# An FFT mixer followed by two MLPs: when the conversions, the transform's sums and the residual's stores are issued

## The chip, the core and the metric

The program runs on one NeuronCore of a Trainium2 chip. The metric is the device time of one execution in microseconds, lower is better. The engines are TensorE (PE), VectorE (DVE), ScalarE (ACT), GpSimd (POOL) and SyncE (SP). Each takes its own instructions strictly in the order in which the program emits them, and waits for semaphores of the others.

## The reference

Three layers follow one another on `x` of 4 x 3136 x 256, in float32:

```python
X = np.fft.rfft(x, axis=1)                         # along the 3136 tokens
x = np.fft.irfft(X * (filt_r + 1j * filt_i), n=3136, axis=1)

h = x.transpose(0, 2, 1) @ U @ V                   # rank 32, along the tokens
u = x + h.transpose(0, 2, 1)
x = u + np.maximum(u @ w_ch1, 0) @ w_ch2           # 256 -> 1024 -> 256

xn = (x - mean) / sqrt(var + 1e-6) * g_ln          # over the 256 channels
out = x + np.maximum(xn @ w_ch1b, 0) @ w_ch2b
```

U, V and the four MLP weights arrive as 64-bit floats, read as pairs of 32-bit words.

## The kernel before

**The arithmetic.** Products that need more precision than one float32r pass are done in three: each operand is split into a high and a low half, and `three` (lines 198 to 201) sums high x high, high x low and low x high on PE. So nearly every tensor has a high half, copied by ACT, and a low half, which DVE subtracts.

**The transform.** `fft(b)` (lines 277 to 357) treats batch b = 1 to 3 as a generator of 36 ticks. The batch's 3136 tokens are 14 pairs of 224 rows. Tick 1 loads; in the first stage (ticks 2 to 16) a tick splits pair i (`split`, lines 296 to 301), multiplies pair i - 1 (`mm1`), and writes the result `ze` to DRAM; POOL's queue loads the tables `ct` (`loadc`, line 290). In the second stage (ticks 19 to 35) a tick splits pair i, multiplies pair i - 1 (`mm2`, lines 313 to 321), whose `filt` (lines 217 to 228) makes `xs` (two copies by ACT, a product by POOL) and `ya` (a product by DVE); then `total` (lines 230 to 237) adds `xs` to `ya` of pair i - 2 on DVE, copies the sum to `yh` on ACT, and subtracts the rest `yl` on DVE; and `back` (lines 239 to 260) multiplies pair i - 3 by the inverse table into `ps`, copies it to `be` on ACT and stores that to `bd[b]`. Tick 36, `finish`, sets `tstk[b]`, from which on units of batch b may be loaded. Batch 0 is transformed ahead of the main loop by other code (class `First`).

**The main loop** (lines 960 to 990) is an order written out by hand. The tokens are 25 blocks of 512 (the last of 256). Each block k has a phase a (first MLP) and a phase b (second MLP), in the order a0 a1 a2 b0 b1 a3 b2 a4 b3 and so on; a phase has 8 steps, one for each 128 of the 1024 hidden channels, 400 steps in all. Step `idx` emits `m1` (six matmuls into `psh`, then ACT's `hh` and DVE's `hl`), `load_to`, perhaps one tick of the transform, the actions of `todo` that are due, and `m2` of step idx - 2, whose last one ends the phase (`end`, lines 655 to 696). In steps 3 and 6 of a phase a, one unit may follow (`unit`, lines 589 to 610): it takes 448 tokens of the transform's result from `bd` to channel-major `ah` and `al` by PE (`psu`), ACT and DVE. The kernel loads a unit (`load_unit`, lines 584 to 587: `ic`, then `wt`) once its batch's `tstk` is set. The first unit of batch 1, unit 7, is due in step 75, and emitting it advances the transform as far as it must.

**The transform's pace** (lines 971 to 975): after step FFT0 = 26 each step adds RATE = 0.75 to a credit while batch 1 is not done, and 0.4 later; when the credit reaches 1, a tick is emitted. Tick 1 falls in step 28, tick 36 in step 74.

**After a phase a** the sum x2 of MLP and residual is finished over the next steps by `todo` entries: DVE's transposes of its halves 3 and 4 steps later (line 675), `x2store` right behind the second one, four transfers to `xd` on SP's queue (lines 698 to 703), `x2load` 4 steps after that (line 708), then statistics on DVE (lines 710 to 734). Phase b ends with DVE's `x2t` (line 686) and the stores of `out` on SP.

**The conversions.** The weights are converted from 64-bit words by generators `to32` (lines 751 to 769). One job goes in segments: ACT writes `h` and `lf`; DVE's `words` makes `t`; POOL multiplies `lf` by `h` and adds it to `t`, named `ct`; `keep(t)` copies the high half (ACT; for w1b a DVE product `wg`, line 832); `last(t)` subtracts the low half, on POOL once `aside` is POOL (line 906), for w2b on DVE. `stagger` (lines 774 to 808) advances all live jobs by one segment per call and, once `brisk` is set just ahead of the main loop (line 961), starts a job every two calls. `CALLS` gives the calls: three in step 0, two in step 1, then one a step up to step 23.

Of the kernel before, what the change touches and what calls it, by code (L numbers as in the profile page):

```python
# [20 lines left out]
P = 128  # L21
# [22 lines left out]
PARTS, UPARTS = (0, 1, 2, 5, 6, 8), 10  # L44
CALLS = (0, 0, 0, 1) + tuple(range(1, 24))
LEAD = 3
FFT0, RATE = 26, 0.75

XTURN, XREAD, XSTAT, XROOT = (3, 4), 8, (10, 11), 12
BW = 32  # L50
# [88 lines left out]
def fft_mixer_kernel(ctx: ExitStack, tc: tile.TileContext, x, U, V, flt, w1, w2, gln, w1b, w2b,  # L139
                     c_fwd32, c_d32, c_e32, c_fwd, c_inv, c_e, c_d, c_w, out):  # L140
    nc = tc.nc
# [21 lines left out]
    def f32(ap):  # L163
        return ap.bitcast(F32)

    def acopy(o, i, scale=1.0):
        nc.scalar.activation(out=o, in_=i, func=AF.Copy, scale=scale)  # L167

    def sub(o, a, b):
        nc.vector.tensor_tensor(out=o, in0=a, in1=b, op=ALU.subtract)  # L170
# [14 lines left out]
    xd = [dram.tile([BLK, D], F32, name=f"xd{k}") for k in range(NBLK)]  # L185
# [6 lines left out]
    NCH = NM // 2  # L192

    def wide(dt, tag, name, w, bufs=2):
        t = fp.tile([PP, 2 * (D + R)], dt, tag=tag, name=name, bufs=bufs)
        return t[:, :2 * w].rearrange("p (a d) -> p a d", a=2)

    def three(o, lh, ll, rh, rl):
        nc.tensor.matmul(o, lh, rh, start=True, stop=False)  # L199
        nc.tensor.matmul(o, lh, rl, start=False, stop=False)  # L200
        nc.tensor.matmul(o, ll, rh, start=False, stop=True)  # L201

    def flat(t):
        return t.rearrange("p a d -> p (a d)")
# [72 lines left out]
    def fft(b):  # L277
        xv = x[b].rearrange("(p m) d -> p m d", m=NM)
        zw = zd[b].rearrange("(q m) w -> q m w", m=NM)
        zr = zd[b].rearrange("(g p) w -> p g w", p=PP)  # L280
        sp = Spectrum(b)
        live, tab, halves = {}, {}, {}

        def load1(i):
            live[i] = wide(F32, "fin", "xt", D, 3)
            nc.sync.dma_start(live[i], xv[:, 2 * i:2 * i + 2, :])

        def loadc(i):
            tab[i] = fp.tile([PP, 2, 2, PP], F32R, tag="ct", name="ct", bufs=2)
            nc.gpsimd.dma_start(tab[i], c_fwd[:, 2 * i:2 * i + 2])  # L290

        def load2(i):
            live[i] = wide(F32, "fin", "zt", D, 3)
            nc.sync.dma_start(live[i], zr[:, 2 * i:2 * i + 2, :])

        def split(i):
            xt = live.pop(i)
            hi, lo = wide(F32R, "fhi", "hi", D), wide(F32R, "flo", "lo", D)
            acopy(hi, xt)
            sub(lo, xt, f32(hi))  # L300
            halves[i] = hi, lo

        def mm1(i):
            ct = tab.pop(i)
            hi, lo = halves.pop(i)
            ze = wide(F32, "fev", "ze", D)
            ps = ps_m.tile([P, 512], F32, tag="m", name="ps1")
            for m in range(2):
                three(ps[:PP, m * D:(m + 1) * D], ct[:, m, 0], ct[:, m, 1], hi[:, m], lo[:, m])
            acopy(flat(ze), ps[:PP])  # L310
            nc.sync.dma_start(zw[:, 2 * i:2 * i + 2, :], ze)

        def mm2(i):
            hi, lo = halves.pop(i)
            ps = ps_m.tile([P, 512], F32, tag="m", name="ps2")
            if i == 0:
                for g in range(2):
                    three(ps[:, g * D:(g + 1) * D], e_sb[:, 1 - g, 0], e_sb[:, 1 - g, 1], hi[:, g], lo[:, g])
            else:
                three(ps, e_sb[:, 0, 0], e_sb[:, 0, 1], flat(hi), flat(lo))  # L320
            sp.filt(i, ps)

        load1(0)
        load1(1)
        loadc(0)
        yield
        for i in range(NCH + 1):
            if i < NCH:
                split(i)
            if i > 0:  # L330
                mm1(i - 1)
            if i + 2 < NCH:
                load1(i + 2)
            if i + 1 < NCH:
                loadc(i + 1)
            yield
        load2(0)
        load2(1)
        sp.load(0)
        for _ in range(2):  # L340
            yield
        for i in range(NCH + 3):
            if i < NCH:
                split(i)
            if 0 < i <= NCH:
                mm2(i - 1)
            if 1 < i <= NCH + 1:
                sp.total(i - 2)
            if i > 2:
                sp.back(i - 3)  # L350
            if i + 2 < NCH:
                load2(i + 2)
            if i + 1 < NCH:
                sp.load(i + 1)
            yield
        sp.finish()
        yield
# [216 lines left out]
    def blen(k):  # L574
        return min(BLK, NTOK - k * BLK)
# [122 lines left out]
    def x2store(k, x2):  # L698

        n = blen(k)  # L700
        for i in range(P // BW):
            nc.sync.dma_start(xd[k].rearrange("(j t) (i c) -> t j i c", t=BW, i=P // BW)[:, :n // BW, i],
                              x2[i * BW:(i + 1) * BW, :n // BW].rearrange("p j c k -> p j (c k)"))

    def x2load(k):
# [37 lines left out]
    def words(s, h, t):  # L743

        hb, tb = h.bitcast(I32), t.bitcast(I32)
        nc.vector.tensor_scalar(out=h, in0=h, scalar1=TOP, scalar2=None, op0=ALU.min)
        nc.vector.tensor_scalar(out=tb, in0=hb, scalar1=3, scalar2=None, op0=ALU.logical_shift_left)
        nc.vector.scalar_tensor_tensor(out=tb, in0=s[:, :, 1], scalar=-0x80000000, in1=tb, op0=ALU.bitwise_and, op1=ALU.bitwise_or)
        nc.vector.tensor_scalar(out=hb, in0=tb, scalar1=-0x800000, scalar2=None, op0=ALU.bitwise_and)

    def to32(i, s, keep, last):


        p, n = s.shape[:2]
        tags = ("xs", "ya") if brisk and i % 2 else ("yh", "yl")
        h, lf = (fp.tile([P, 512], F32, tag=tag, name=f"c{tag}", bufs=3 if tag == "ya" else 2)[:p, :n] for tag in tags)
        nc.scalar.activation(out=h, in_=s[:, :, 1].bitcast(F32), func=AF.Abs, scale=2.0 ** -112)
        nc.scalar.activation(out=lf, in_=s[:, :, 0].bitcast(U32), func=AF.Copy, scale=2.0 ** -52)
        yield
        t = fp.tile([P, 2 * (D + R)], F32, tag=("fhi", "flo")[i % 2], name="ct", bufs=2)[:p, :n]  # L760
        words(s, h, t)
        yield
        nc.gpsimd.tensor_tensor(out=lf, in0=lf, in1=h, op=ALU.mult)
        nc.gpsimd.tensor_tensor(out=t, in0=t, in1=lf, op=ALU.add)
        yield
        keep(t)
        yield
        last(t)
        yield

    after = []
    aside, brisk = nc.vector, False

    def stagger(jobs):

        words, live, fetched = {}, [], 0
        after.clear()

        def fetch(n):
            nonlocal fetched  # L780
            while fetched < min(n, len(jobs)):
                words[fetched] = jobs[fetched][0]()
                fetched += 1

        def advance():
            nonlocal live
            while after:
                after.pop()()
            live = [g for g in live if next(g, 0) is None]

        for n in range(4):
            fetch(n + 1)
            yield
        for i in range(len(jobs) + 4):
            if brisk:
                advance()
            if i < len(jobs):
                live.append(to32(i, words.pop(i), *jobs[i][1:]))
                next(live[-1])
            yield  # L800
            advance()
            if brisk:
                fetch(i + 3)
            yield
            if not brisk:
                advance()
                fetch(i + 3)
                yield
# [73 lines left out]
    with tc.manual_schedule():  # L882
# [6 lines left out]
        def chain():  # L889
            for b in range(1, NB):  # L890
                yield from fft(b)

        first = First()
        pr = stagger([w_job("w1", w1, 0, "wt"), w_job("w1", w1, 1, "wt"), v_job(0), v_job(1)] + [w_job(nm, w, j) for nm, w, j in (
            ("w2", w2, 0), ("w1", w1, 2), ("w1", w1, 3), ("w2", w2, 1), ("w2", w2, 2),
            ("w2", w2, 3), ("w1b", w1b, 0), ("w1b", w1b, 1), ("w2b", w2b, 0), ("w1b", w1b, 2), ("w1b", w1b, 3),
# [64 lines left out]
        brisk = True  # L961
# [61 lines left out]
```

## Time and profile before

| | |
|---|---|
| median of 3 runs | 1402.79 us (1402.31 to 1405.51) |
| the profiled execution | 1402.46 us, its span 1400.7 us |
| PE busy | 1358.4 us (97%), 7678 matmuls |
| DVE, ACT, POOL busy | 802.0 (57%), 549.8 (39%), 173.9 us (12%) |
| granted clock of PE, mean | 0.989 |
| the chain that ended last | PE 82%, DVE 4%, ACT 2%, DMA 1% |
| DMA | 152.29 MB, mean 109 GB/s |

The profile is of one execution; the sum in the prediction is made against that one's 1402.46 us. Matmuls overlap one another, so PE's busy time is a union of overlapping spans: where it is full, a matmul follows the last without a gap, and where it is not, PE waited. "A <- B" says that A stood idle until B's instruction was done. A wait of an engine that is not late for anything costs nothing.

### The profile page before, as it was taken

Reading aid. Unit: us, or ns where it says so; the run is one execution under the profiler, and the core shown is the slowest. Engines: PE = TensorE matmul, PEld = TensorE weight load, DVE = VectorE, ACT = ScalarE, POOL = GpSimd, SP = SyncE. Lnnn points to the kernel's source line nnn. Section 1 sums busy time; section 2 is a strip of 40 time slices with the busy share of each in tenths; the row PEclk is TensorE's granted clock in tenths of the full one; section 3 lists DMA queues with packets and bytes.
Section 4 is the critical chain, followed back from the end, with each engine's and each line's share of the span. In section 5 each row is a group of like instructions: output and inputs, shape, how many; then the busy total and the mean of one; then the engine's idle time right before and its main releaser. Section 6 shows DMA issues by size and latency. Waiting matters only on the chain.

```text
span 1400.7 us, 20122 instructions
## 1 busy us (share of the span) xinstructions
PE 1358.4 (97%) x7678; PEld 1173.4 (84%) x7678; DVE 802.0 (57%) x1533; ACT 549.8 (39%) x1048; POOL 173.9 (12%) x170
## 2 busy tenths in 40 slices
PE   8888899999899999999999999999999999999998
PEld 8576789887788888888888887888888888888898
DVE  4777974478554455667554445766444444444444
ACT  4864434366433334445333334544322222222222
POOL 3737511022100001111000001111000000000000
PEclk9899999999999999999999999999999999999999
DMA  9735237555526424444345344353122013201111
GB/s 282 246 77 162 75 82 196 166 163 166 158 56 159 125 89 129 120 142 130 74 118 152 91 131 131 98 168 84 58 65 65 16 49 84 65 16 31 46 46 38
DMA packets 140576, 152.29 MB, mean 109 GB/s; under 512 B 61472, under 2 KB 117696, under 8 KB 140384
## 3 DMA queue, kind: packets, MB, share of 16 engines
q1 hardware_dynamic: 131840, 132.37, 33.4%
q0 software_dynamic: 7776, 17.44, 5.1%
q8 instruction: 60, 0.98, 0.3%
q10 hardware_dynamic: 864, 1.20, 0.2%
q14 instruction: 36, 0.29, 0.1%
HBM read 103.44 MB, written 47.54 MB: 108 GB/s over the span
## 4 chain that ended last, share of the span: by engine, by line
PE 82%; DVE 4%; ACT 2%; DMA 1%; issue 1%; SPq 0%; POOL 0%; DVEq 0%; ACTq 0%; POOLq 0%
PE psh L624 36%; PE pso L653 6%; PE pso L652 6%; PE pso L651 6%; PE pso L643 6%; PE pso L644 5%; PE pso L645 5%; PE psu L595 3%; PE ps L199 2%; PE ps L201 2%; PE ps L200 2%; DVE ya L234 1%; PE psu L597 1%; ACT xs L167 1%; PE pt L255 1%
## 5 line engine op out<-in xcount | busy, mean ns | idle before, releaser
L628 DVE SCALAR_TENSOR_TENSOR hl<-psh,hh 128x512 fp32r<-128x512 f32 (+1 forms) x400 | 271.0, 679 | 427.1 <-ACT hh L627 426.7
L627 ACT ACTIVATE hh<-psh 128x512 fp32r<-128x512 f32 (+1 forms) x400 | 234.9, 588 | 604.5 <-PE psh L624 603.8
L624 PE MATMUL psh<-ah,wb 128*128 128x512 f32 (+1 forms) x800 | 276.7, 387 | 0.2 <-DVE hl L628 0.2
L651 PE MATMUL pso<-wb,hh 128*128 128x256 f32 x784 | 221.1, 282 | 1.1 <-DVE x L666 1.1
L653 PE MATMUL pso<-wb,hl 128*128 128x256 f32 x784 | 221.8, 283 | 0.0
L652 PE MATMUL pso<-wb,hh 128*128 128x256 f32 x784 | 221.7, 283 | 0.0
L624 PEld LDWEIGHTS psh<-ah,wb 128*128 128x128 f32 x800 | 150.3, 189 | 28.0 <-DVE hl L628 0.8
L624 PE MATMUL psh<-ah,w1h 128*128 128x512 f32 (+1 forms) x400 | 157.6, 394 | 5.4 <-DVE hl L628 5.4
L643 PE MATMUL pso<-hh,w2h 128*128 128x512 f32 (+1 forms) x400 | 155.0, 388 | 6.8 <-DVE x2t L686 3.5
L651 PEld LDWEIGHTS pso<-wb,hh 128*128 128x128 f32 x784 | 149.7, 191 | 7.5 <-DVE x L666 1.3
L624 PE MATMUL psh<-al,w1h 128*128 128x512 f32 (+1 forms) x400 | 155.8, 390 | 0.0
L624 PE MATMUL psh<-al,wb 128*128 128x512 f32 (+1 forms) x400 | 155.5, 389 | 0.0
L624 PE MATMUL psh<-ah,w1l 128*128 128x512 f32 (+1 forms) x400 | 155.1, 388 | 0.0
L644 PE MATMUL pso<-hl,w2h 128*128 128x512 f32 (+1 forms) x400 | 154.5, 386 | 0.0
L652 PEld LDWEIGHTS pso<-wb,hh 128*128 128x128 f32 x784 | 149.7, 191 | 5.5
L645 PE MATMUL pso<-hh,w2l 128*128 128x512 f32 (+1 forms) x400 | 154.2, 386 | 0.0
L653 PEld LDWEIGHTS pso<-wb,hl 128*128 128x128 f32 x784 | 149.8, 191 | 0.0
L227 POOL TENSOR_TENSOR xs<-xs,ft 128x512 f32<-128x512 f32 x42 | 55.1, 1312 | 391.4 <-ACT xs L167 383.8
L643 PEld LDWEIGHTS pso<-hh,w2h 128*128 128x128 f32 x400 | 75.4, 188 | 22.5 <-DVE x2t L686 4.4
L624 PEld LDWEIGHTS psh<-ah,w1h 128*128 128x128 f32 x400 | 75.9, 190 | 20.0 <-DVE hl L628 7.5
L624 PEld LDWEIGHTS psh<-ah,w1l 128*128 128x128 f32 x400 | 75.6, 189 | 16.0
L645 PEld LDWEIGHTS pso<-hh,w2l 128*128 128x128 f32 x400 | 75.2, 188 | 15.4
(170 smaller groups left out, 1932.2 us busy)
## 6 DMA issues: line engine op xcount, KB each, us to landing
ft<-flt SPq DMA_DIRECT2D x42, 512.0 KB, 4.4
xd<-x SPq DMA_DIRECT2D x96, 128.0 KB, 2.8
x2t<-xd SPq DMA_DIRECT2D x24, 512.0 KB, 4.5
wt<-bd SPq DMA_DIRECT2D x24, 448.0 KB, 5.8
out<-x2t SPq DMA_DIRECT2D x84, 128.0 KB, 2.1
xt<-x SPq DMA_DIRECT2D x42, 224.0 KB, 3.7
zd<-ze SPq DMA_DIRECT2D x42, 224.0 KB, 2.8
zt<-zd SPq DMA_DIRECT2D x42, 224.0 KB, 3.2
```

Of the source, the lines that this page charges most:

```text
L199: nc.tensor.matmul(o, lh, rh, start=True, stop=False)
L227: (cross or nc.gpsimd).tensor_tensor(out=xs, in0=xs, in1=ft[:, :, 1], op=ALU.mult)
L595: nc.tensor.matmul(ps[:, m:UN:UW], t[:, m, dh * P:(dh + 1) * P], ic[:, m, :], start=m == 0, stop=False, skip_group_check=True)
L624: nc.tensor.matmul(ps[:, :n], w[:, kt, fs], a[:, kt, :n], start=j == 0, stop=j == 3 * KT - 1)
L627: nc.scalar.activation(out=hh[:, :n], in_=ps[:, :n], func=AF.Relu)
L628: nc.vector.scalar_tensor_tensor(out=hl[:, :n], in0=ps[:, :n], scalar=0.0, in1=f32(hh[:, :n]), op0=ALU.max, op1=ALU.subtract)
L643: nc.tensor.matmul(o, wh[:, f, ds], hh[:, :n], start=f == 0, stop=False)
L644: nc.tensor.matmul(o, wh[:, f, ds], hl[:, :n], start=False, stop=False)
L645: nc.tensor.matmul(o, wl[:, f, ds], hh[:, :n], start=False, stop=f == FT - 1)
L651: nc.tensor.matmul(o, hh[:, cs], wh[:, f, :], start=f == 0 and c % 2 == 0, stop=False, skip_group_check=True)
L652: nc.tensor.matmul(o, hh[:, cs], wl[:, f, :], start=False, stop=False, skip_group_check=True)
L653: nc.tensor.matmul(o, hl[:, cs], wh[:, f, :], start=False, stop=f == FT - 1, skip_group_check=True)
```

## The change

It has four parts. (1) In `to32`, when `brisk` is set, an empty segment comes between POOL's two operations and `keep`, and `stagger` runs one turn longer. (2) In the second stage's tick `total(i - 2)` is emitted ahead of `split(i)` and `mm2(i - 1)` and not behind them. (3) FFT0 goes from 26 to 22 and RATE from 0.75 to 0.72: tick 1 falls in step 24. (4) The four stores of `x2store` are issued by POOL's queue and no longer by SP's.

```diff
--- before.py
+++ after.py
@@ -44,7 +44,7 @@
 PARTS, UPARTS = (0, 1, 2, 5, 6, 8), 10
 CALLS = (0, 0, 0, 1) + tuple(range(1, 24))
 LEAD = 3
-FFT0, RATE = 26, 0.75
+FFT0, RATE = 22, 0.72
 
 XTURN, XREAD, XSTAT, XROOT = (3, 4), 8, (10, 11), 12
 BW = 32
@@ -340,12 +340,12 @@
         for _ in range(2):
             yield
         for i in range(NCH + 3):
+            if 1 < i <= NCH + 1:
+                sp.total(i - 2)
             if i < NCH:
                 split(i)
             if 0 < i <= NCH:
                 mm2(i - 1)
-            if 1 < i <= NCH + 1:
-                sp.total(i - 2)
             if i > 2:
                 sp.back(i - 3)
             if i + 2 < NCH:
@@ -699,7 +699,7 @@
 
         n = blen(k)
         for i in range(P // BW):
-            nc.sync.dma_start(xd[k].rearrange("(j t) (i c) -> t j i c", t=BW, i=P // BW)[:, :n // BW, i],
+            nc.gpsimd.dma_start(xd[k].rearrange("(j t) (i c) -> t j i c", t=BW, i=P // BW)[:, :n // BW, i],
                               x2[i * BW:(i + 1) * BW, :n // BW].rearrange("p j c k -> p j (c k)"))
 
     def x2load(k):
@@ -763,6 +763,8 @@
         nc.gpsimd.tensor_tensor(out=lf, in0=lf, in1=h, op=ALU.mult)
         nc.gpsimd.tensor_tensor(out=t, in0=t, in1=lf, op=ALU.add)
         yield
+        if brisk:
+            yield
         keep(t)
         yield
         last(t)
@@ -791,7 +793,7 @@
         for n in range(4):
             fetch(n + 1)
             yield
-        for i in range(len(jobs) + 4):
+        for i in range(len(jobs) + 5):
             if brisk:
                 advance()
             if i < len(jobs):
```

## Rows read from the trace of the kernel before

**Rows 1.** By stretch: us; PE, PEld, DVE, ACT, POOL busy (count); clock; DMA share; GB/s
```profile
98.00:186.00 88.00, 79.54 (x362) 62.73 (x360) 74.81 (x119) 43.01 (x79) 51.22 (x44) 0.98 0.37 102
186.00:290.00 104.00, 104.00 (x635) 93.10 (x635) 56.02 (x118) 42.69 (x82) 8.37 (x14) 1.00 0.56 152
290.00:366.00 76.00, 72.69 (x394) 59.40 (x393) 59.76 (x96) 45.45 (x84) 17.83 (x15) 1.00 0.58 166
366.00:388.00 22.00, 17.53 (x95) 15.15 (x94) 7.82 (x15) 5.88 (x11) 0.00 (x0) 0.92 0.76 198
558.00:604.00 46.00, 42.75 (x247) 36.32 (x246) 30.41 (x47) 22.04 (x41) 6.45 (x5) 1.00 0.47 135
842.00:872.00 30.00, 27.25 (x157) 23.65 (x156) 17.07 (x28) 12.12 (x23) 3.89 (x3) 0.94 0.41 117
```

**Rows 2.** Waits from 98 to 186 us: total us, times, longest
```profile
ACT w2h L167 <- POOL ct L764: 7.7, 3, 3.7
...
PE psh L624 <- DVE hl L628: 4.6, 5, 2.0
...
DVE wg L832 <- POOL ct L764: 4.3, 2, 2.2
...
PE pso L643 <- DVE x L666: 3.2, 2, 1.7
```

**Rows 3.** PE's waits over the whole span, the same columns
```profile
PE psu L595 <- DMA wt<-bd: 4.5, 1, 4.5
...
PE pso L643 <- DVE x2t L686: 3.5, 2, 2.3
...
PE ps L199 <- ACT be L167: 3.3, 8, 1.0
...
PE psu L595 <- ACT be L167: 1.4, 2, 1.0
...
PE pso L651 <- DVE x L666: 1.1, 1, 1.1
```

**Rows 4.** Timeline of ACT around one tick: start us, us, [idle before <-releaser]
```profile
854.49 0.60 ACT L627 ACTIVATE hh<-psh 128x512 fp32r<-128x512 f32 x1 [2.22 <-PE psh L624]
...
855.64 1.20 ACT L167 ACTIVATE xs<-ps 64x512 f32<-64x512 f32 x2
...
858.79 0.63 ACT L167 ACTIVATE yh<-ya 128x512 fp32r<-128x512 f32 x1 [1.95 <-DVE ya L234]
```

**Rows 5.** Timeline of DVE around the same tick, the same columns
```profile
855.12 0.69 DVE L628 SCALAR_TENSOR_TENSOR hl<-psh,hh 128x512 fp32r<-128x512 f32 x1 [2.13 <-ACT hh L627]
...
856.87 0.69 DVE L226 TENSOR_TENSOR ya<-ps,ft 128x512 f32<-128x512 f32 x1 [0.46 <-ACT xs L167]
...
857.48 1.28 DVE L234 TENSOR_TENSOR ya<-ya,xs 128x512 f32<-128x512 f32 x1
...
860.06 1.65 DVE L686 SCALAR_TENSOR_TENSOR x2t<-pso,ln,x2t 128x256 f32<-128x256 f32 x4
```

**Rows 6.** Instructions of line 234: count, ns min/median/max, first and last start
```profile
L234 DVE TENSOR_TENSOR ya<-ya,xs x42: 681/1275/1284, 289.7 to 977.2; 128x512 f32<-128x512 f32 x42
```

**Rows 7.** Timeline of ACT, two ticks in neighbouring steps
```profile
297.34 0.63 ACT L167 ACTIVATE yh<-ya 128x512 fp32r<-128x512 f32 x1 [1.95 <-DVE ya L234]
...
302.70 0.63 ACT L167 ACTIVATE yh<-ya 128x512 fp32r<-128x512 f32 x1 [2.01 <-DVE ya L234]
```

**Rows 8.** Timeline of SP's queue at step 75
```profile
376.61 0.54 SPq L708 DMA_DIRECT2D x2t<-xd  x1
```

**Rows 9.** Chain that ended last, from 376 to 386: start us, us, what
```profile
377.83 6.20 DMA wt<-bd
```

**Rows 10.** The page's DMA issues: count, KB each, median us to landing
```profile
wt<-bd SPq DMA_DIRECT2D x24, 448.0 KB, 5.8
```

**Rows 11.** Instructions of line 702 on SP's queue, columns of rows 6
```profile
L702 SPq DMA_DIRECT2D xd<-x x100: 302/504/1460, 159.5 to 1380.5; - x100
```

**Rows 12.** POOL's issues of line 290: count, busy us, mean ns, idle before
```profile
L290 POOL DMA_DIRECT2D ct<-c_fwd x42 | 22.0, 524 | 324.3 <-PE ps L201 321.2 <-DMA ct<-c_fwd 3.0
```

## The prediction

> **What bounds the kernel now.** I read the page's busy shares first, then PE by stretches, then what ended PE's idle time in the stretches where it has any, then single ticks in the timeline. PE is the bound nearly everywhere: from 186 to 290 us it is busy for 104.00 of 104.00 us, so nothing can be won there [rows 1]. The reader should look for the five stretches that are not full: 98 to 186 (steps 0 to 23, where the weights are converted; 8.46 us idle), 290 to 366 (second stage of transform 1; 3.31), 366 to 388 (step 75; 4.47), 558 to 604 and 842 to 872 (second stages of transforms 2 and 3; 3.25 and 2.75). Together 22.2 us. In three of them the granted clock is 0.98, 0.92 and 0.94 instead of 1.00: 0.02 of 88, 0.08 of 22 and 0.06 of 30 us are 1.7 us each that PE lost at the lower level (1.2 of 2.4 GHz) behind a stall. So about 27 us is all that this change could touch; PE's idle time before 98 us and at the end is outside it.
>
> The waits say who keeps PE. In the conversions [rows 2] PE waits for `hl` of DVE (4.6 us, 5 times, longest 2.0) and for a `pso` bank that DVE's residual sum must read (3.2, twice, longest 1.7). DVE and ACT in their turn stand still for POOL's `ct`: ACT 7.7 us in three waits of its copy to `w2h`, DVE 4.3 in two. Both are in-order, so `hh` and `hl` queue behind these waits. Later PE waits behind the transform's tick [rows 3]: 8 times for the bank that ACT's `be` copy frees (3.3 us), twice for DVE's `x2t` (3.5), once for `x` (1.1), twice for `be` ahead of a unit (1.4), and once for the load of `wt` (4.5).
>
> **Part 1, the empty tick.** A conversion now leaves one tick, a step of PE, between POOL's two products and the copy that reads them. The waits for `ct` that ACT and DVE have now were at most 3.7 and 2.2 us [rows 2], about one step, so nearly all of each goes. Of PE's 7.8 us of stalls in [rows 2] I give the longest of each kind (2.0 and 1.7) to DVE being slow beside POOL, which stays; the other 4.1 us I take as won. Ends: 0, if POOL is then late by another tick, and 7.8.
>
> **Part 2, the sum ahead of the split.** In a tick of the second stage ACT copies `hh` (started 854.49) and `hi`, then `xs` from 855.64, then stands until DVE's sum is done and copies `yh` at 858.79 [rows 4]. DVE's product of 856.87 and the sum behind it (1.28) come after `xs`; `yl` follows `yh`, and only then comes the `x2t` that PE needs, at 860.06 [rows 5]: 5.57 us from the start of `hh`. After the change the sum follows `hl` at once. It then no longer runs beside POOL's product for the same pair; its fastest case is 0.68, the median 1.28 [rows 6]. New chain: 0.63 to the start of `hl`, 0.69 for it, 0.68 sum, 0.63 `yh`, 0.65 `hi`, 1.20 `xs`, 0.69 product: 5.17, less some 0.2 by which neighbours overlap, so 4.97 to `x2t`. That is only 0.6 shorter: nothing is taken out but the slow half of the sum, since `yh` now stands ahead of `xs` on ACT and `xs` waits for it. With ticks in neighbouring steps the loop from `yh` to `yh` is 5.36 [rows 7] and shrinks by about 0.5 in the same way. So of the 8 stalls of 0.4 on average in transform 1, all but the longest (1.0) go: 3.3 - 0.5 = 2.8. Of the five stalls in transforms 2 and 3 four lose 0.6 and the small one of the `be` pair all its 0.4: 2.8. Ends: 0 (the new order keeps `xs` as late as it makes `yh` early), and 9.3, all the stalls of this kind.
>
> **Part 3, the transform from step 22 at 0.72.** It starts four steps earlier, but at the lower rate its 36 ticks take 50 steps and not 48; and sums of 0.72 in floating point end just short of 36 after 50 steps, so the last tick comes in step 73, where it now comes in 74. The load of unit 7 can therefore be issued in step 74 and not in 75. On SP that is ahead of the block's `x2t` load, which now stands at 376.61 [rows 8], ahead of `wt` at 377.83 [rows 9]. SP itself is held by the stores of `out` until about 376.6 in both orders, so `wt` is issued only some 0.6 us sooner (its `ic` still goes first), and without 512 KiB ahead of it, which are 2.6 us at the 198 GB/s of this stretch [rows 1]. Ends: 1.0, if it lands at the median of 5.8 [rows 10], 383.0 and not 384.0; and 0.6 + 2.6 = 3.2. I take the middle, 2.1. The four added steps of first-stage ticks lie where PE has no idle time; the sparser rate costs nothing there either. If that cover were gone (DVE late from the conversions at step 24), it would show as `hl` waits between 186 and 200 us.
>
> **Part 4, the residual's stores on POOL.** 100 transfers of 512 rows of 256 bytes leave SP, where issuing one takes 0.50 [rows 11], and go to POOL. SP only gains freedom that no PE wait asks for: 0 won. On POOL each now waits for DVE's transpose, and behind it stand the conversions' products (block 0, step 14), the table loads `ct` (block 2, step 30) and the products `xs` (from block 3). The trace has no store from POOL. Its nearest row is a load of 112 rows, 0.52 [rows 12]; by rows, 512 would take 2.4. I take 0.52, the nearer in kind to SP's 0.50, so 2.1 us a block. POOL is busy for 51 of 88 us in the conversions and 18 of 76 in the dense transform [rows 1], so 2.1 fits between: 0. Ends: 0 and, at 2.4 each, the first rival.
>
> **Sum.** 4.1 + 2.8 + 2.8 + 2.1 = 11.8. Of the three stretches at the low clock I count one as gone, since each stands behind a stall that the terms above shorten: 1.7. Total 13.5. The profiled execution took 1402.46 us, 0.3 below the median of 1402.79, so 1389.0.
>
> **The rivals.**
> POOL's stores turn into the bound (slower). At 2.4 us each, a block's four hold POOL for 9.6. From about 1.2 each the four outlast a dense tick's 5 us and this begins to decide. At step 14 the conversions are then late by 9.6 less the one empty tick of 2.8: 7 us. The `ct` load at step 30 comes late by about 2; and in seven later ticks (block 3, two blocks of transform 2, three of transform 3, and one step beside a unit) the sum waits some 2 us for `xs`: 14. That is 23 against 13.5 won: 1412. For it speaks that these transfers have over four times the rows of any that POOL issues now; against it, that SP's issue of the same rows costs no more than that of others. The Trainium skill, in "SBUF — State Buffer" (the note on the DVE-blocks-DMA trap), says that POOL writes such a transfer's descriptors itself, and that a two-port operation on DVE locks it out meanwhile: 620 ns alone, 3100 beside DVE. It advises against this move. By its factor of five, as an estimate, the 0.52 of the row would be 2.6, much the same end as by rows. No run here shows it for stores yet.
>
> The sum in front only moves the wait (same). `yh` waits for the sum, and `hi` and `xs` wait behind it; if DVE's `hl` is late, the whole tick is. Then part 2 gives 0, the clock 0 and the conversions half: 1402.5 - 2.0 - 2.1 = 1398.4.
>
> The conversions stay bound by DVE beside POOL: part 1 gives 0: 1393.
>
> All stalls of the ticks and the small ones of the conversions go: 7.8 + 9.3 + 3.2 + 3.4 = 23.7, so 1379.
>
> That the empty tick does nothing is excluded by the code: it is yielded whenever the flag is set at that moment, which holds from step 0 on.
>
> **How the numbers follow.** Forecast 0.50, POOL bound 0.08, sum moved only 0.15, conversions unchanged 0.15, all gone 0.12. A measurement of this kernel can tell about 0.3% (4.2 us) from no change, so faster begins below 1398.6. Faster: 0.50 + 0.15 + 0.12 and a fifth of the moved sum, 0.03: 0.80; same 0.12; slower 0.08. The range leaves out the rival with POOL and half of the case where all goes: 1381 to 1401.
>
> **What would show it.** Right: in 98 to 186 the waits of ACT and DVE for `ct` are near 0 and PE's idle time is about 4; the sum's median is 0.68; the waits of `ps` for `be` shrink below 0.6 us in all; PE's wait for `wt` is 2 to 3; POOL's stores are near 0.5 each. Wrong: a POOL issue of over 1.2; a wait of DVE's sum for `xs`, which is new; `xs` on ACT starting over 3.5 us after `hh`; or PE waiting for `ct<-c_fwd` in the first stage.

## The result and the profile of the changed kernel

The changed kernel takes 1414.99 us (median of 4 runs, 1414.37 to 1415.93), the kernel before 1402.81 in the same rounds: ratio 1.0083, 95% interval 1.0066 to 1.0101. It is slower by 12 us where 13.5 less were forecast. The profiled execution took 1414.51 us, its span is 1412.7.

First the changed kernel by stretch, columns as in [rows 1]. The steps lie later here, so the bounds are moved to the same steps: conversions, the rest of the first stage, second stage of transform 1, the load of `wt`, second stage of transform 2.

```profile
99.00:194.00 95.00, 81.52 (x361) 63.00 (x361) 78.67 (x124) 43.66 (x81) 53.72 (x46) 0.96 0.35 97
194.00:306.00 112.00, 110.12 (x670) 97.61 (x669) 63.52 (x124) 49.05 (x93) 17.46 (x26) 1.00 0.56 155
306.00:381.00 75.00, 70.06 (x377) 57.11 (x377) 50.47 (x89) 42.14 (x76) 17.91 (x19) 1.00 0.51 148
381.00:400.00 19.00, 15.26 (x81) 13.01 (x80) 5.69 (x11) 4.18 (x8) 1.63 (x3) 0.92 0.73 197
566.00:612.00 46.00, 44.22 (x246) 37.23 (x244) 29.06 (x46) 23.95 (x43) 9.06 (x9) 1.00 0.46 134
```

Steps 0 to 23 took 88 us before and 95 now, with 13.5 us of idle PE where there were 8.5, at a mean clock of 0.96 where it was 0.98. The second stage has 4.9 us idle in 75, before 3.3 in 76.

Then PE's waits over the whole span of the changed kernel (total us, times, longest), to be held against [rows 2, 3]:

```profile
PE psh L624 <- DVE hl L628: 9.1, 9, 2.2
PE psu L595 <- ACT be L167: 5.8, 3, 2.2
...
PE ps L199 <- ACT be L167: 3.8, 6, 1.2
...
PE psu L595 <- DMA wt<-bd: 3.6, 1, 3.6
PE psw L850 <- DVE al L170: 3.2, 1, 3.2
```

Three things are to be seen: the waits for `hl` grew (over the whole span before they were 5.6 us in seven), a unit now waits for `be` three times for 5.8 us (twice for 1.4 before), and `psw`, the product with `ones` in `center`, waits 3.2 us for DVE. That last wait is new. The load of `wt` still keeps PE for 3.6 us.

What the change was to take away is mostly gone all the same. The first row is from the waits of the changed kernel from 99 to 194 us, the second its sum on DVE (count, ns min/median/max), the third its stores on POOL, the same columns:

```profile
ACT w2h L167 <- POOL ct L764: 4.0, 1, 4.0
```
```profile
L234 DVE TENSOR_TENSOR ya<-ya,xs x42: 674/681/684, 290.8 to 983.0; 128x512 f32<-128x512 f32 x42
```
```profile
L702 POOL DMA_DIRECT2D xd<-x x100: 582/651/729, 165.4 to 1392.5; - x100
```

The 7.7 us of `w2h` are 4.0, the 4.3 of `wg` have no row left, the sum takes 0.68 and not 1.28, a store takes POOL 0.65. The waits that the forecast counted on PE did not go with them.

### The profile page after: what moved, and what is told of

Its sections match the earlier page's. It is cut to its first block, busy times and chain, and to the rows that moved or that the text cites. A ratio compares the mean times of both kernels' runs of the same rounds, so it can differ in the third digit from the quotient of the medians.

```text
span 1412.7 us, 20182 instructions
## 1 busy us (share of the span) xinstructions
PE 1359.1 (96%) x7678; PEld 1172.6 (83%) x7678; DVE 794.1 (56%) x1533; ACT 555.0 (39%) x1048; POOL 238.9 (17%) x270
## 4 chain that ended last, share of the span: by engine, by line
PE 81%; DVE 7%; ACT 4%; DMA 3%; issue 3%; SPq 1%; POOL 1%; ACTq 0%; DVEq 0%; POOLq 0%
PE psh L624 35%; PE pso L653 6%; PE pso L652 6%; PE pso L651 6%; PE pso L643 5%; PE pso L644 5%; PE pso L645 5%; PE psu L595 3%; PE ps L199 2%; PE ps L201 2%; PE ps L200 2%; ACT xs L167 1%; DVE hl L628 1%; DMA x<-x 1%; PE psu L597 1%
## 5 line engine op out<-in xcount | busy, mean ns | idle before, releaser
L702 POOL DMA_DIRECT2D xd<-x x100 | 64.6, 654 | 502.2 <-DVE x L675 499.6
L643 PEld LDWEIGHTS pso<-hh,w2h 128*128 128x128 f32 x400 | 75.5, 189 | 18.9 <-DVE x2t L686 3.2
```

Of the source, the lines that this page charges most:

```text
L643: nc.tensor.matmul(o, wh[:, f, ds], hh[:, :n], start=f == 0, stop=False)
L702: nc.gpsimd.dma_start(xd[k].rearrange("(j t) (i c) -> t j i c", t=BW, i=P // BW)[:, :n // BW, i], x2[i * BW:(i + 1) * BW, :n // BW].rearra ...
```

## The experiments

All times are medians of several runs, ratios are to the kernel before on the same chip (its medians were 1403.1 to 1403.8). To see where each kernel loses time, I worked out one more figure from each trace: for every matmul, the time from its start to the next one's start beyond what its columns take back to back at the higher clock (0.228 us for 512 columns, 0.113 for 256), added up by steps. It holds PE's waits and the half-speed stretches together. The stretch before step 0 is left out: its code is the same in all kernels, but the profiled execution of before lost 59.9 us there and all the others 60.8 to 62.9, so 1 to 3 us of each difference between spans is chance. A row is of one execution; those of one_start and early_sum_all were the slowest of theirs, 2.5 and 3.6 us over their medians, so their losses read a little high.

| us lost by PE in steps | 0-8 | 8-12 | 12-20 | 20-24 | 24-52 | 52-60 | 60-74 | 74-80 | 80-160 | 160-224 | 224-400 | sum |
|---|---|---|---|---|---|---|---|---|---|---|---|---|
| before | 6.6 | 4.5 | 7.1 | 0.7 | 4.5 | 2.8 | 6.0 | 7.2 | 15.5 | 13.6 | 20.8 | 89.3 |
| changed | 7.3 | 6.9 | 6.1 | 6.0 | 4.3 | 8.0 | 4.8 | 6.8 | 15.0 | 13.4 | 21.0 | 99.7 |
| one_empty | 7.4 | 7.6 | 5.8 | 4.0 | 4.3 | 2.7 | 6.0 | 7.9 | 15.5 | 12.9 | 21.0 | 95.1 |
| empty_not_w1b | 7.3 | 4.2 | 7.9 | 0.0 | 4.3 | 2.7 | 5.9 | 8.5 | 15.5 | 12.9 | 21.1 | 90.4 |
| one_sum | 6.7 | 4.5 | 6.8 | 0.7 | 4.7 | 2.6 | 5.9 | 6.9 | 16.6 | 14.5 | 21.0 | 90.8 |
| early_sum | 6.6 | 4.5 | 7.1 | 0.7 | 4.6 | 1.7 | 1.7 | 8.8 | 12.0 | 10.7 | 21.0 | 79.3 |
| one_start | 6.6 | 4.5 | 7.1 | 0.7 | 8.9 | 8.4 | 5.4 | 8.0 | 15.9 | 11.8 | 21.0 | 98.3 |
| start_r75 | 6.6 | 4.5 | 7.0 | 0.7 | 9.1 | 5.0 | 4.1 | 1.0 | 13.8 | 9.5 | 25.1 | 86.5 |
| start_r75_pool | 6.6 | 4.5 | 7.2 | 0.7 | 6.2 | 5.1 | 4.1 | 1.0 | 13.9 | 9.9 | 25.2 | 84.5 |
| one_pool | 6.6 | 4.5 | 7.2 | 0.7 | 5.6 | 3.2 | 6.0 | 8.6 | 15.6 | 12.9 | 21.1 | 92.1 |
| early_sum_all | 7.3 | 7.6 | 6.1 | 6.0 | 4.3 | 3.1 | 1.6 | 8.0 | 12.1 | 9.6 | 21.0 | 86.9 |
| best_a | 6.7 | 4.5 | 7.2 | 0.7 | 6.2 | 1.8 | 1.6 | 1.0 | 11.6 | 9.5 | 21.7 | 72.4 |
| best_b | 6.7 | 4.5 | 6.8 | 0.7 | 4.5 | 2.1 | 1.6 | 0.9 | 11.4 | 9.0 | 21.7 | 69.9 |
| less_dve | 4.4 | 1.8 | 3.5 | 0.0 | 4.5 | 2.7 | 6.0 | 8.0 | 15.5 | 12.8 | 21.1 | 80.4 |
| less_pool | 4.7 | 1.8 | 7.5 | 0.0 | 4.3 | 2.8 | 5.9 | 7.6 | 15.5 | 12.9 | 21.2 | 84.2 |

The changed kernel's 10.4 us over before are 6.7 in steps 8 to 24 (2.4 - 1.0 + 5.3) and 5.2 in steps 52 to 60; the other steps give back 1.5.

### Each part alone on the kernel before

The edits are the four hunks of the change, one at a time.

**one_empty**, 1409.16 us, ratio 1.0042 (1.0027 to 1.0057).

> Only the empty tick of part 1 on the kernel before. Theory A (the empty tick does its work on the waits for ct, and what the change lost in steps 8 to 23 comes from the store of block 0 on POOL and from the transform's earlier start): 2 to 4 us faster than before. Rival B (the empty tick itself costs: the later phases of a job come one step later, so that center's psw matmul falls behind a unit, and PE waits for DVE there): 1 to 6 us slower, with an al wait of some 3 us at about 147 us as in the profile after.

Rival B came. The loss is in steps 8 to 12 (3.1) and 20 to 24 (3.3). The first, in PE's timeline of this kernel (start us, us, [idle before <-releaser]), and DVE's of the same moment:

```profile
144.52 0.45 PE L597 MATMUL psu<-v_sb,tk 96*128 96x448 f32 x1
148.16 2.05 PE L850 MATMUL psw<-wg,ones 128*128 128x512 f32 x2 [3.19 <-DVE al L170]
```
```profile
141.69 2.33 DVE L746 TENSOR_SCALAR cxs<-cxs 128x512 f32<-128x512 f32 x1
...
145.59 0.68 DVE L628 SCALAR_TENSOR_TENSOR hl<-psh,hh 128x512 fp32r<-128x512 f32 x1
146.19 0.68 DVE L672 TENSOR_TENSOR x<-x,al 128x512 f32<-128x512 f32 x1
146.79 0.35 DVE L170 TENSOR_TENSOR al<-psu,ah 128x192 fp32r<-128x192 f32 x1
```

`center` comes one call later, so its product now stands on PE behind a unit and needs the PSUM buffer that the unit's `al` frees. DVE reaches that `al` only behind a conversion's whole `words` and a residual. Before, the product started at 138.20, ahead of the unit.

**one_sum**, 1406.23 us, 1.0024 (1.0013 to 1.0035).

> Only the sum and the copies yh and yl ahead of the next split, on the kernel before. Theory A (yh, which waits for DVE's sum, now holds up hi, xs and be behind it on ACT; the tick with DVE's other work ahead of hl grows from 5.36 to about 5.58): slower by 2 to 6 us, most of it in 290 to 366 us, with waits of a unit for be in transforms 2 and 3. Rival B (the order is worth what the prediction said, and the loss is the conversions' alone): 3 to 6 us faster.

Theory A by the time, but not by the place: transform 1 is unchanged, and transforms 2 and 3 lose 1.1 and 0.9 us. `be` keeps units for 3.7 us in all (1.4 before). Nor did the tick grow, as theory A had it: the median from `hh` to `be` fell (Part 2 below).

**one_start**, 1410.06 us, 1.0050 (1.0035 to 1.0065).

> Only the transform from step 22 at rate 0.72, on the kernel before. Theory A (four first-stage ticks fall into the conversions' last steps, and the DVE work of both together keeps PE waiting for hl; the load of unit 7 comes earlier, but issued at 391.80 in the profile after it saves under 1 us of PE's wait): 0 to 4 us slower. Rival B (as the prediction said): 2 us faster.

The dearest part alone, and neither theory had its size or its place: 4.4 us in steps 24 to 28, where the first load of the transform is late, and 5.6 in steps 52 to 60. ACT's timeline and SP's of this kernel:

```profile
191.67 0.60 ACT L627 ACTIVATE hh<-psh 128x512 fp32r<-128x512 f32 x1 [2.12 <-PE psh L624]
195.53 0.63 ACT L167 ACTIVATE hi<-xt 112x512 fp32r<-112x512 f32 x1 [3.26 <-DMA xt<-x]
196.06 0.58 ACT L627 ACTIVATE hh<-psh 128x512 fp32r<-128x512 f32 x1
```
```profile
189.12 2.17 SPq L702 DMA_DIRECT2D xd<-x  x4
191.34 1.83 SPq L286 DMA_DIRECT2D xt<-x  x3
```

The first `xt` stands on SP behind the residual's four stores, which wait for DVE's transposes; tick 2, a step later, has ACT copy it to `hi`. DVE's `lo` waits for that copy, and right behind `lo` stands the next block's residual sum `x`, for which PE waits. The waits of DVE and PE there:

```profile
DVE lo L170 <- ACT hi L167: 3.2, 1, 3.2
...
PE pso L651 <- DVE x L666: 2.5, 1, 2.5
```

The load took 3.5 to 4.3 us to land.

**one_pool**, 1406.37 us, 1.0023 (1.0014 to 1.0033).

> Only the residual's stores on POOL, on the kernel before. Theory A (each store takes POOL 0.65 as in the profile after, and hides everywhere but in block 0 at step 14, where it stands ahead of the conversions' products): 0 to 3 us slower, all of it before 190 us. Rival B (the stores also delay xs and ct in the transforms): 4 to 10 us slower, spread over 290 to 872 us.

Theory A by the time; the places are other ones: 1.1 in steps 24 to 52 (the next residual sum `x` waits 2.1 us for the stores, before 0.7) and 1.4 in steps 74 to 80, about the load of `wt`. The latter is within what the length of a half-speed stretch there varies: 6.8 us in this trace, 3.4 in that of before.

The four losses add up to 18.4 us by the medians, the changed kernel lost 12: the parts overlap. The largest overlap is seen in the table: one_start's 4.4 us in steps 24 to 28 are absent in the changed kernel, whose stores are on POOL.

### Which piece of each part does it

**early_sum**, 1392.91 us, 0.9917 (0.9901 to 0.9934). Only DVE's addition moves:

```diff
+        def add(self, i):
+            ya, xs = self.y[i]
+            nc.vector.tensor_tensor(out=ya, in0=ya, in1=xs, op=ALU.add)
...
         for i in range(NCH + 3):
+            if 1 < i <= NCH + 1:
+                sp.add(i - 2)
             if i < NCH:
                 split(i)
```

> On the kernel before, only DVE's sum goes ahead of the next split; ACT's yh and DVE's yl stay behind the products. Theory A (the sum alone on one_sum cost 0.2% because yh stands on ACT ahead of hi, xs and be and waits for the sum; left where it was, it starts as soon as xs is done, and be comes sooner than in both kernels): the units' waits for be vanish, the bank waits for be shrink, 2 to 5 us faster than before. Rival B (the place of yh does not matter, the sum ahead of lo delays lo and PE with it): within 2 us of one_sum, that is 1 to 4 us slower than before.

Theory A, at more than twice its gain: 10.7 us. The same work on ACT in the changed kernel and in early_sum, two timelines of a dense second stage:

```profile
299.94 0.59 ACT L627 ACTIVATE hh<-psh 128x512 fp32r<-128x512 f32 x1
302.63 0.63 ACT L167 ACTIVATE yh<-ya 128x512 fp32r<-128x512 f32 x1 [2.10 <-DVE ya L234]
303.17 0.61 ACT L167 ACTIVATE hi<-zt 112x512 fp32r<-112x512 f32 x1
303.81 1.20 ACT L167 ACTIVATE xs<-ps 64x512 f32<-64x512 f32 x2
305.03 0.60 ACT L167 ACTIVATE be<-ps 112x512 f32<-112x512 f32 x1
305.52 0.59 ACT L627 ACTIVATE hh<-psh 128x512 fp32r<-128x512 f32 x1
```
```profile
294.66 0.60 ACT L632 ACTIVATE hh<-psh 128x512 fp32r<-128x512 f32 x1 [2.28 <-PE psh L629]
295.15 0.62 ACT L167 ACTIVATE hi<-zt 112x512 fp32r<-112x512 f32 x1
295.80 1.20 ACT L167 ACTIVATE xs<-ps 64x512 f32<-64x512 f32 x2
297.02 0.63 ACT L167 ACTIVATE yh<-ya 128x512 fp32r<-128x512 f32 x1
297.56 0.58 ACT L167 ACTIVATE be<-ps 112x512 f32<-112x512 f32 x1
```

With `yh` in front ACT stands idle for 2.10 us until DVE's sum, and `be` starts 5.09 after `hh`; this is one of the slow ticks, the median of the 42 is 4.36 (4.83 before). With `yh` behind `xs` the sum is done by then: no idle time, `be` 2.90 after `hh`, which is also the median. In the changed kernel DVE had this to do before that sum:

```profile
300.06 0.70 DVE L675 STREAM_TRANSPOSE x<-x 128x512 f32<-128x512 f32 x1
300.69 0.65 DVE L170 TENSOR_TENSOR al<-x,ah 128x512 fp32r<-128x512 f32 x1
301.26 0.68 DVE L628 SCALAR_TENSOR_TENSOR hl<-psh,hh 128x512 fp32r<-128x512 f32 x1
301.86 0.68 DVE L234 TENSOR_TENSOR ya<-ya,xs 128x512 f32<-128x512 f32 x1
```

**empty_not_w1b**, 1405.45 us, 1.0010 (1.0001 to 1.0019).

```diff
-        if brisk:
+        if brisk and i not in (10, 11, 13, 14):
             yield
```

> On the kernel before, the empty tick for all conversions but the four of w1b, whose products feed center. Theory A (PE's 3.2 us behind psw come from center being one tick later and so behind a unit): that wait goes and the kernel is 2.5 to 4 us faster than one_empty; the 3.4 us lost in steps 20 to 24 remain, because the last job still ends a tick later. Rival B (all of the empty tick's loss comes from DVE's work being shifted against the residuals, psw is only where it shows): the loss moves to another wait of the same steps, within 1.5 us of one_empty.

3.7 us faster than one_empty, as theory A had it, but its second clause was wrong: the loss of steps 20 to 24 went too, so it belonged to `w1b`, and not to the last job. There PE waited in one_empty for `hl` (1.2 and 2.2 us) and not for `psw`; the first of the two stands behind ACT's copy of the second `center`, which waits for DVE (3.20 before):

```profile
176.43 1.23 ACT L167 ACTIVATE wb<-wg 128x512 fp32r<-128x512 f32 x2 [5.01 <-DVE wg L854]
```

What is left is that the empty tick wins nothing: 18.9 us lost in steps 0 to 24 before, 19.4 now, although ACT's waits of `w2h` for `ct` fell from 7.7 to 4.0 us here too.

**start_r75**, 1401.25 us, 0.9985 (0.9975 to 0.9994): `FFT0, RATE = 22, 0.75`.

> On the kernel before, the transform from step 22 at the old rate of 0.75. In one_start PE lost 4.35 us more in steps 24 to 28 (ACT's copy of xt to hi waits 3.3 for a load that stands on SP behind the residual's stores) and 5.6 more in steps 52 to 60. Theory A (the first loss belongs to the start at 22, the second to the rate: at 0.75 each fourth step has no tick, and those are the steps in which a unit is made, at 0.72 ticks fall on them): the first loss stays, 4 us; the second goes; and the load of wt, whose last tick comes in step 70 and not 74, is there in time, 4.5 won plus up to 3 of the low clock: 1 slower to 3 faster than before. Rival B (the second loss comes from the earlier place of the second stage against the blocks' ends, whatever the rate): 5 us slower again in steps 52 to 60, 2 to 5 us slower than before in all.

Theory A: steps 24 to 28 lose the same as in one_start, but steps 52 to 74 lose 4.7 less than there, and the load of `wt` is in time, 1.0 for 7.2 in steps 74 to 80. From step 22 at 0.75 ticks come in steps 56, 57, 58, 60, 61, 62 and so on: each fourth step is free, and 59, in which a unit is made, is one of them. At 0.72 a tick falls on 59, and one_start lost 3.1 us there, start_r75 and before 0.9. Steps 160 to 224 lose 4.1 less than before and 224 to 400 lose 4.3 more: transform 3's second stage lies a little later, no more.

**start_r75_pool**, 1398.52 us, 0.9959 (0.9944 to 0.9973).

> As start_r75, with the residual's stores on POOL as well. Theory A (the stores on SP are what keeps the first load of xt back at step 24): the wait of hi for xt goes, and steps 24 to 28 lose under 1.5 us more than before; 2 to 5 us faster than start_r75. Rival B (xt is late for another reason, the transfers of step 23 themselves): steps 24 to 28 lose 4 us as in one_start, and POOL adds its own 2 to 3 us, slower than start_r75.

Theory A: 2.7 us faster than start_r75, and `hi` waits for `xt` no more. Steps 24 to 28 still lose 1.7 over before, a little more than expected, with a wait of PE for the table that POOL loads:

```profile
PE ps L199 <- DMA ct<-c_fwd: 1.5, 1, 1.5
```

### What binds the conversions

**less_dve**, 1395.24 us, 0.9945 (0.9930 to 0.9960), and **less_pool**, 1399.31 us, 0.9971 (0.9960 to 0.9983):

```diff
-        nc.vector.scalar_tensor_tensor(out=tb, in0=s[:, :, 1], ...
+        if not brisk:
+            nc.vector.scalar_tensor_tensor(out=tb, in0=s[:, :, 1], ...
```
```diff
-        nc.gpsimd.tensor_tensor(out=lf, in0=lf, in1=h, op=ALU.mult)
+        if not brisk:
+            nc.gpsimd.tensor_tensor(out=lf, in0=lf, in1=h, op=ALU.mult)
```

> The kernel before, where from step 0 on each conversion leaves out DVE's operation that joins the sign bit to the high word (0.69 us each; the converted weights lose their signs). Theory A (steps 0 to 23 are bound by DVE, which is busy for 82 of 88 us of 98 to 186, so that the empty tick took waits away that cost nothing): PE's losses of 18.9 us in steps 0 to 24 fall by 3 to 6, 3 to 6 us faster than before. Rival B (POOL's products bind, and DVE only waits for them): within 2 us of before.

> The kernel before, where from step 0 on each conversion leaves out POOL's product of the low word with the high word (1.28 us each; the converted weights are wrong in their low bits). Theory A (DVE binds): the waits for ct vanish as with the empty tick, and the kernel is within 2 us of before but for DVE operations that no longer run beside POOL at double length, at most 3 us faster. Rival B (POOL binds): 4 to 8 us faster, more than less_dve.

Eleven conversions have these operations in the main loop. DVE's eleven took 9.5 us before (0.69 each at the least, up to 1.67); without them the kernel is 7.9 us faster, more than expected. POOL's eleven took 14.3; without them it is 3.8 faster, between the two theories. A microsecond of DVE is worth 0.8 of the kernel's, a microsecond of POOL a quarter. Both operations stand in the chain that leads to `ct`; since the longer one is worth less, it is not that chain that binds. With less DVE, PE's waits from 98 to 186 us for `hl` and for the residual are down from 4.6 and 3.2 [rows 2] to:

```profile
PE pso L643 <- DVE x L666: 1.0, 1, 1.0
PE psh L624 <- DVE hl L628: 0.9, 2, 0.6
```

So DVE binds, while ACT's `w2h` still waits 4.9 us for `ct`. POOL's product costs what it does in part by slowing DVE beside it (last section); how the 3.8 us split between that and the waits was not tried.

### Inside the whole change, and a better kernel

**all_but_sum** (part 2 undone), 1414.29 us, 1.0073 (1.0057 to 1.0090), **all_but_empty** (part 1 undone), 1410.31 us, 1.0046 (1.0029 to 1.0063), and **early_sum_all** (the changed kernel with part 2 as in early_sum), 1399.50 us, 0.9968 (0.9956 to 0.9981).

> The changed kernel with the sum and its copies back behind the products: three of the four parts. Theory A (yh ahead of hi, xs and be costs here what it cost alone, 2 to 4 us): 1411 to 1413 us, with the units' waits for be back near 2 us. Rival B (with the other three parts in place the second stage loses by the rate alone, the order of the sum adds nothing): 1414 to 1416.

> The changed kernel without the empty tick. Theory A (the parts lose in different places: the empty tick 3 us at psw in steps 8 to 12 and 3 to 5 in steps 20 to 24): 5 to 8 us faster than the changed kernel, 1407 to 1410, with steps 20 to 24 at under 1 us of losses. Rival B (with the transform's start at 22 DVE is late in steps 20 to 28 in any case): 1411 to 1414.

> The changed kernel, but of the sum's step only DVE's addition goes ahead of the split, yh and yl stay behind the products. Theory A (part 2 as written failed by the place of yh alone, and early_sum won 10 us by it): 8 to 11 us faster than the changed kernel, 1404 to 1407, its loss against before then being that of the conversions (steps 8 to 24) and of the ticks that the rate of 0.72 puts next to units. Rival B (at 0.72 the ticks' collisions eat the gain): within 4 us of the changed kernel.

In place of the 2.9 us that it cost alone, the early `yh` costs under 1 here (rival B, within the spread of both): the ticks that the rate puts beside units lose as much in either order, 8.1 us in steps 52 to 60 without part 2 and 8.0 with it. The empty tick costs 4.7, a little under theory A's range, and steps 20 to 24 are back at 0.7 us. Leaving `yh` where it was wins 15.5 us, beyond theory A: steps 52 to 60 fall from 8.0 to 3.1, 60 to 74 from 4.8 to 1.6, 80 to 224 from 28.4 to 21.7. With `xs` and `be` early, even the ticks beside units cost little.

**best_a** (early_sum, start at 22 with 0.75, stores on POOL), 1386.98 us, 0.9876 (0.9860 to 0.9893), and **best_b** (early_sum, `FFT0, RATE = 24, 0.75`, stores on SP), 1384.04 us, 0.9855 (0.9841 to 0.9870).

> early_sum with the transform from step 22 at the rate 0.75 and the residual's stores on POOL (start_r75_pool). Theory A (the gains lie in different places: 4 to 5 us of early_sum in the second stage of transform 1, 3 each in transforms 2 and 3; 6 us of start_r75 at the load of wt): 1387 to 1391 us. Rival B (transforms 2 and 3 gain the same time only once, since start_r75 already won there): 1391 to 1394.

> early_sum with the transform from step 24 at the rate 0.75, the stores left on SP. Theory A (the last tick comes in step 72 and not 74, so wt can be loaded ahead of its unit; with the first tick in step 26 the first load of xt has one step more after the residual's stores than in one_start): 4 to 7 us faster than early_sum, 1386 to 1389 us. Rival B (xt still lands behind its copy, as in one_start): 4 us are lost in steps 24 to 28, 1390 to 1393.

Theory A in both, best_b a little better than its range. best_b has a tick on step 59 too (its free steps are 57, 61, 65 and so on), and loses 2.1 us in steps 52 to 60. By stretch, as [rows 1], from 290 us on:

```profile
290.00:366.00 76.00, 75.99 (x423) 64.16 (x423) 58.77 (x97) 46.94 (x86) 16.84 (x14) 1.00 0.59 170
366.00:388.00 22.00, 22.00 (x117) 18.95 (x116) 11.92 (x30) 7.74 (x15) 0.00 (x0) 1.00 0.51 148
```

The second stage and the load of `wt` cost PE next to nothing any more, and the clock of both stretches is 1.00. best_b is 19.8 us (1.5%) faster than the kernel before and needs none of parts 1 and 4.

## Why the prediction was wrong

**Reading the bound: right where it was counted from PE.** The stretches named are the places where there was time to win: best_b won 19.8 us, nearly all of it in the four outside the conversions. By the prediction's count these held 17.2 (13.8 idle and two low-clock stretches), so it was a little low; PE's busy time, in which matmuls overlap, can hide the shortest gaps.

**Part 1 (4.1 won; measured alone 5.8 lost).** The failed step is the one from POOL's `ct` to PE: "the other 4.1 us I take as won". ACT and DVE waited for `ct`, but PE waited for `hl` and `x`, which DVE makes, and DVE had as much to do without the waits: less_dve shows it. So the rival "the conversions stay bound by DVE beside POOL" was the true mechanism, and priced at nothing won; it lacked the second failed step, that a shift by a call moves everything behind it: `center` slid behind a unit (empty_not_w1b: 3.7 of the 5.8 us).

**Part 2 (5.6 won; alone 2.9 lost).** The chain itself came out much as forecast: the median from `hh` to `be` over the 42 ticks fell from 4.83 to 4.36 us, and the sum to 0.68. Only where the dense stage has transposes and halves of a residual ahead of `hl`, which the chain "0.63 to the start of `hl`, 0.69 for it, 0.68 sum, 0.63 `yh`" left out, is the sum ready 2.0 and not 1.4 us after `hh` ends (rows above), and the loop there takes 305.52 - 299.94 = 5.58 and not some 4.9; such ticks were slow before too.

The step that failed is what the shorter chain was to do for PE: "all but the longest (1.0) go" and "four lose 0.6". The chain was followed to `x2t` and from `yh` to `yh`, but not to the PSUM bank that `xs` sets free, although the harmful piece was in the text ("`yh` now stands ahead of `xs` on ACT and `xs` waits for it"). In the code `ps` and `psu` take two banks in turn, so a unit's first product needs the bank that `xs` and, behind it, DVE's `ya` have read. The median from `hh` to `xs` grew from 1.14 to 3.13 us. ACT in a tick of transform 2 with a unit behind it, before and in the changed kernel, and PE's wait in the latter:

```profile
595.15 0.60 ACT L627 ACTIVATE hh<-psh 128x512 fp32r<-128x512 f32 x1 [3.06 <-PE psh L624]
596.30 1.20 ACT L167 ACTIVATE xs<-ps 64x512 f32<-64x512 f32 x2
599.97 0.58 ACT L167 ACTIVATE be<-ps 112x512 f32<-112x512 f32 x1
```
```profile
608.11 0.60 ACT L627 ACTIVATE hh<-psh 128x512 fp32r<-128x512 f32 x1 [2.88 <-PE psh L624]
611.25 1.19 ACT L167 ACTIVATE xs<-ps 64x512 f32<-64x512 f32 x2
612.46 0.60 ACT L167 ACTIVATE be<-ps 112x512 f32<-112x512 f32 x1
```
```profile
PE psu L595 <- ACT be L167: 1.8, 1, 1.8
```

`be` comes sooner after `hh` and `xs` 2.0 us later. The wait is put down to `be`, but `ya` ends within 0.1 us of it. Before, the unit's first product did not wait and its second 1.0. In one_sum such a wait of 1.8 stands in transforms 2 and 3 each, and each is followed by a half-speed stretch (601.7 and 871.4 us), where before had one. In transform 1 PE's waits of `ps` for `be`, forecast to fall from 3.3 to 0.5, are 3.0 in one_sum and 3.8 in the changed kernel. The rival "the sum in front only moves the wait" named this. early_sum, in which `xs` is back at 1.14, shows that the addition alone, with the two copies left behind, takes 10.7 us off; `yh` and `yl` were moved together in every run, so what `yl` alone does is not shown.

**Part 3 (2.1 won; alone 6.7 lost).** Two readings failed. "The four added steps of first-stage ticks lie where PE has no idle time; the sparser rate costs nothing there either": the first load of `xt` is a DMA of the moved step, and I passed it over when looking at the queues; on SP it is behind the stores. And the rate was looked at for its length and last tick only, not for the steps on which its ticks fall: 5.6 us in steps 52 to 60, of which 3.4 go with 0.75 and all with early_sum beside it (best_a). The gain at `wt` was mis-sized too: SP issued it at 391.80, behind the stores of `out`, and PE waited 3.6 (forecast 2 to 3). SP's timeline of the changed kernel:

```profile
388.55 2.51 SPq L694 DMA_DIRECT2D out<-x2t  x4
391.15 0.54 SPq L581 DMA_DIRECT2D ic<-c_inv  x1
391.80 0.38 SPq L587 DMA_DIRECT2D wt<-bd  x1
```

A last tick in step 73 is not early enough to be ahead of those stores; one in step 72 is, as best_b shows, where the load is issued at 368.11 and the stores follow at 370.46.

**Part 4 (0; alone 3.0 lost).** The price, 0.52 a store, was near (0.65), and the rival at 2.4 each did not occur: that it gave 1412, near the result, is chance. The Trainium skill, in "SBUF — State Buffer" (the note on the DVE-blocks-DMA trap and the section behind it), gives some five times the time, 3100 for 620 ns, for a transfer that POOL issues while DVE runs a `tensor_copy`; the longest issue of the 100 stores here took 0.73, so no run shows it. Alone the move cost time because the stores come later and the next `x` waits for them (2.1 us for 0.7), a wait that the prediction did not follow. But "SP only gains freedom that no PE wait asks for" held for the kernel before alone: with the start at 22 it is worth 2.7 us (start_r75_pool against start_r75), because it frees the way for `xt`.

**The clock (1.7 won).** There are four half-speed stretches where before had three: 147.9 us, behind the wait for `psw`, 185.4, 397.0 and 881.7, each behind a wait of PE of 1.8 to 3.6 us. So 1.7 us were lost and not won.

**What stays open.** Why one_sum costs 2.9 us alone and under 1 inside the change was read from the table and not tried further; nor was the part of DVE's slow operations in the 5.8 us of one_empty taken apart.

## What to carry to other kernels

An in-order engine that waits for something costs nothing until the engine that binds needs its next result: before a wait is removed, follow it to the bound engine, and test whether the producer on that path has any slack. When one instruction is moved forward, move that one alone: what depends on it (here a copy on another in-order engine) should stand where its input is already there, behind work that is ready; and ask of the work that it pushes back which buffer that work sets free. And a pace of background work is a pattern against the foreground's steps, so look at which steps it hits and at what its first and last transfers stand behind, not only at its length.

## What the runs showed of the hardware that was not expected

Operations of DVE that usually take 0.4 us took up to 2.33 beside one of POOL: in one_empty `L746`, median 0.415, ran from 141.69 to 144.02, beside POOL's `uh_sb` product of 2.56:

```profile
141.18 2.56 POOL L461 TENSOR_TENSOR uh_sb<-uf,uh_sb 128x896 fp32r<-128x896 f32 x1
```

It ended 0.3 us after POOL's did. The Trainium skill, "SBUF — State Buffer", section "Who interferes with whom", says of a DVE operation in a two-port mode (`tensor_scalar` is among those that can enter one) and one of POOL that whichever issues first holds the shared port pair for the whole instruction and the other is blocked; these rows agree, though none shows the mode. The prediction saw that DVE is slow beside POOL, but not that one operation could be stretched to more than five times its length.

A load of `xt` that SP issues behind waiting stores holds up matmuls that do not use it: 3.3 us of waiting on ACT became 2.5 us of PE's by way of `lo` and `x`, and with the half-speed stretch of 3.4 us that followed (198.9 us in one_start) some 4.4 us of its losses. Waits of PE as short as 1.8 us (`psu`, changed kernel, stretch at 881.7) were followed by such a stretch, but not all: one of 2.2 for `hl` at 185.8 us in one_empty was not. Each stretch of 3.4 us costs half of itself, 1.7.
